# Attention and channel mix on one core: q and k loaded as 16-bit by GpSimd and turned on VectorE, scores in 32x64 tiles, a new order

## The chip, the cores and the metric

The kernel runs on one core of a Trainium2 chip. A core has a matrix engine (TensorE, PE in the profile, with its weight loads on a row of their own, PEld), VectorE (DVE), ScalarE (ACT), GpSimd (POOL), SyncE (SP), and 16 DMA engines that move data between the chip's memory (HBM) and the core's on-chip memory. TensorE reads on-chip memory (SBUF) and writes PSUM, eight banks of 512 32-bit numbers for each of 128 partitions. The metric is the device time of one execution in microseconds (us), lower is better. The kernel before took 272.23 us, the median of three executions of 269.08, 272.96 and 272.23 us.

## The reference

Eight batches of eight heads of blockwise causal attention (576 positions, 64 numbers per head, blocks of 64 positions), and then a channel mix (RWKV style) on the 512 joined channels. Cut to what matters:

```python
scores = scale * np.matmul(q, k.transpose(0, 1, 3, 2))        # (8, 8, 576, 576)
mask = pos[:, None] // 64 >= pos[None, :] // 64
attn = softmax(np.where(mask, scores, -1e9))
x = np.matmul(attn, v)      # heads joined: (8, 576, 512)
x_prev = x shifted by one position
xk = mu_k * x + (1 - mu_k) * x_prev
xr = mu_r * x + (1 - mu_r) * x_prev
k = np.maximum(xk @ w_k, 0)             # 512 -> 1024
out = sigmoid(xr @ w_r) * (k * k @ w_v) # 1024 -> 512
```

All inputs and the output are 32-bit; the tensors q, k and v are 9.4 MB each and the output as much.

## The kernel before

Every engine executes its own list of instructions in order, and waits on the others through semaphores. The lists are written by hand: a plan holds tasks with their buffers (`RINGS` gives the number of buffers of each kind), the table `ORDER` gives the order in which the tasks are issued, and the string `PLACE` says which of DVE, ACT and POOL does a task that any of them could do.

Attention of one batch has these stages.

- **Load and turn.** TensorE needs q and k with the head dimension on the partitions. Batches 0 to 3 (`LONGS`) load long rows of 2304 bytes (`add_long`, 288 KB a transfer), cast them to bf16 into `t_nl`, transpose 64x64 blocks on TensorE against the identity (L371) into PSUM, and copy these to `t_qkt` (L262, L268). Batches 4 to 7 load rows of 256 bytes (`add_qk`), cast them into `t_nb`, and transpose them by DMA (L318). The values v are loaded and cast into `t_vo` (`add_v`).
- **Scores.** `add_scores` multiplies k by q, transposed, into `t_s` (three PSUM buffers of two banks). From batch 1 on, a unit of four heads is made of matmuls on 64x64 tiles of the array (L489), four of them on different quarters. ACT takes the exponential into `t_e` (L517, 1024 or 640 numbers a partition). Batch 0 has units of its own, with 64x128 tiles (L499).
- **Values.** `add_av` sums the exponentials (S, L577) and multiplies them by the values (T, A and B, L586: 64x32 tiles), in `t_s` buffers too. DVE turns the sums (L620), takes reciprocals (L626), turns those back (L634), and scales the result into `t_xt` (norm, L642 and L650). Batch 0 has two groups with a form of their own (`add_av0`).
- **Mix.** `add_mix` makes x minus x_prev (L742, or L739 on ACT) and from it `t_xk` and `t_xr` (L766, L770), laid out in chunks of 512 positions. 576 is not a multiple of 512, so most mixes are split in two.

The channel mix runs over nine chunks of 512 positions (c), in PSUM buffers `t_mm` (two banks): `add_pk` (L794: 8 times 4 matmuls of 128x128 by 512 columns, relu at L804 or L806, square at L812 or L814), `add_pr` (L828, tanh at L836), `add_pv` (L854, product at L864, store at L872). TensorE's instructions at L279 (`unread`) are matmuls whose result nobody reads, put in by `ORDER` at the start and in the first 40 us. SP issues every load, store and DMA transpose, 181 rows in all.

## Time and profile before

| | before |
|---|---|
| executions | 269.08, 272.96, 272.23 us (median 272.23) |
| span of the profiled execution | 269.2 us (its own time is not given apart; the span equals the fastest of the three) |
| PE busy | 247.1 us (92%), 3700 matmuls |
| DVE busy | 196.7 us (73%) |
| ACT busy | 184.8 us (69%) |
| POOL busy | 92.3 us (34%) |
| SP's DMA queue | 110208 packets, 75.5% of 16 engines' span |
| chain that ended last | PE 62%, DMA 13%, DVE 8%, ACT 7%, SP's issuing 4% |

An engine's busy time is the time in which any of its instructions runs; instructions overlap, so the sum over groups is larger than that. The chain that ended last follows the work back from the last instruction to what released it. "Window" below is a stretch of the span, in us from its start. The median of the executions is 3.0 us above the span.

### The profile page before, as it was taken

How to read it: one execution, taken by the hardware profiler on the slowest of the kernel's cores; microseconds unless marked ns; L12 is line 12 of the kernel's file. 1: busy time of each engine (PE TensorE's matmuls, PEld its weight loads, DVE VectorE, ACT ScalarE, POOL GpSimd, SP SyncE). 2: the span in 40 equal slices, each digit the busy share in tenths (PEclk: the TensorE clock that was granted, in tenths of full speed). 3: DMA queues.
4: the chain of work that ended last, by engine and by line, in shares of the span. 5: the costliest groups of instructions: out<-in, count | busy, mean ns of one | idle time of the engine just before them, and what ended most of it. 6: DMA issues, size and time to landing. Idle time of an engine off the chain costs nothing.

```text
span 269.2 us, 8792 instructions
## 1 busy us (share of the span) xinstructions
PE 247.1 (92%) x3700; PEld 123.4 (46%) x3700; DVE 196.7 (73%) x354; ACT 184.8 (69%) x270; POOL 92.3 (34%) x123
## 2 busy tenths in 40 slices
PE   7879779899899996789899999699999999999995
PEld 3544336444446444334354445345444544444442
DVE  1597696999888976266968969588985599943432
ACT  4869588788786885399569886695788563661440
POOL 3555614731337311365155103413403350140310
PEclk9988799999999999999999999999999999999999
DMA  7999997899999697998999899889932201202213
GB/s 217 391 205 315 268 228 209 261 259 228 220 239 223 166 226 162 207 209 225 201 198 225 195 223 207 199 192 219 194 104 78 80 4 39 80 0 79 78 56 144
DMA packets 110249, 48.83 MB, mean 181 GB/s; under 512 B 98816, under 2 KB 99072, under 8 KB 110208
## 3 DMA queue, kind: packets, MB, share of 16 engines
q1 hardware_dynamic: 110208, 48.25, 75.5%
q8 instruction: 29, 0.48, 0.8%
q14 instruction: 12, 0.10, 0.1%
HBM read 33.56 MB, written 9.44 MB: 160 GB/s over the span
## 4 chain that ended last, share of the span: by engine, by line
PE 62%; DMA 13%; DVE 8%; ACT 7%; SPq 4%; issue 3%; POOL 1%; DVEq 0%; ACTq 0%; POOLq 0%
PE t_mm L854 18%; PE t_mm L794 15%; PE t_mm L828 10%; PE t_s L489 5%; PE t_s L586 5%; DMA t_vl<-in_v_dram 4%; ACT t_e L517 4%; SPq L251 4%; DMA out_dram<-t_o 2%; DMA t_ld<-in_q_dram 2%; PE t_s L577 2%; DMA t_qkt<-t_nb 2%; PE t_s L371 2%; DMA t_ld<-in_k_dram 2%; ACT t_kr L804 2%
## 5 line engine op out<-in xcount | busy, mean ns | idle before, releaser
L517 ACT ACTIVATE t_e<-t_s 128x1024 f16<-128x1024 f32 (+1 forms) x96 | 88.9, 977 | 15.4 <-PE t_s L489 13.4
L794 PE MATMUL t_mm<-t_xk,WK 128*128 128x512 f16 x288 | 67.8, 379 | 4.1 <-ACT t_kr L804 2.7
L854 PE MATMUL t_mm<-WV,t_k 128*128 128x512 f16 (+1 forms) x296 | 66.4, 374 | 0.2 <-DVE t_k L814 0.2
L804 ACT ACTIVATE t_kr<-t_mm 128x512 f32<-128x512 f32 x61 | 36.2, 599 | 29.2 <-PE t_mm L794 23.1
L814 POOL TENSOR_TENSOR t_k<-t_kr 128x512 f16<-128x512 f32 x26 | 29.0, 1128 | 60.5 <-ACT t_kr L804 36.8
L794 PEld LDWEIGHTS <-WK 128*128 128x128 f16 x288 | 26.7, 97 | 37.0 <-issue 8.2
L854 PEld LDWEIGHTS <-t_k 128*128 128x128 f16 x296 | 27.7, 98 | 33.8 <-issue 2.3
L864 DVE SCALAR_TENSOR_TENSOR t_o<-t_t,t_mm 128x512 f32<-128x512 f32 (+1 forms) x37 | 24.8, 670 | 20.4 <-PE t_mm L854 13.0
L828 PE MATMUL t_mm<-WR,t_xr 128*128 128x512 f16 x144 | 35.9, 379 | 0.7 <-ACT t_kr L804 0.7
L770 DVE SCALAR_TENSOR_TENSOR t_xk<-t_d,MUK,t_xt 128x384 f16<-128x384 f32 (+7 forms) x56 | 30.8, 563 | 7.2 <-POOL t_d L742 7.2
L770 DVE SCALAR_TENSOR_TENSOR t_xr<-t_d,MUR,t_xt 128x384 f16<-128x384 f32 (+7 forms) x56 | 32.7, 599 | 0.0
L836 ACT ACTIVATE t_t<-t_mm 128x512 f32<-128x512 f32 x36 | 21.4, 598 | 16.1 <-PE t_mm L828 13.3
L489 PE MATMUL t_s<-t_qkt 64*64 64x64 bf16 (+7 forms) x560 | 25.4, 291 | 3.3 <-DMA t_qkt<-t_nb 3.3
L742 POOL TENSOR_TENSOR t_d<-t_xt 128x576 f32<-128x576 f32 x16 | 19.0, 1193 | 23.7 <-DVE t_xk L770 12.0
L814 DVE TENSOR_TENSOR t_k<-t_kr 128x512 f16<-128x512 f32 x24 | 18.1, 755 | 8.5 <-ACT t_kr L804 8.4
L586 PE MATMUL t_s<-t_e,t_vo 64*32 64x64 f16 (+7 forms) x1120 | 20.8, 284 | 1.1 <-POOL t_vo L268 1.1
L828 PEld LDWEIGHTS <-t_xr 128*128 128x128 f16 x144 | 13.5, 97 | 17.8 <-issue 3.0
L489 PEld LDWEIGHTS <-t_qkt 64*64 64x64 bf16 x560 | 12.4, 106 | 17.5 <-issue 10.2
L268 POOL CAST t_vo<-t_vl 128x576 f16<-128x576 f32 (+1 forms) x17 | 12.9, 761 | 20.9 <-DMA t_vl<-in_v_dram 20.9
L586 PEld LDWEIGHTS <-t_vo 64*32 64x32 f16 x1120 | 14.6, 92 | 9.1 <-issue 3.2
L268 DVE COPY t_qkt<-t_s 128x576 bf16<-128x576 bf16 x18 | 13.1, 752 | 7.3 <-PE t_s L371 6.6
L268 POOL CAST t_nl<-t_ld 128x576 bf16<-128x576 f32 x18 | 11.8, 666 | 19.0 <-DMA t_ld<-in_k_dram 13.4
(73 smaller groups left out, 242.5 us busy)
## 6 DMA issues: line engine op xcount, KB each, us to landing
out_dram<-t_o SPq DMA_DIRECT2D x35, 256.0 KB, 2.9
t_vl<-in_v_dram SPq DMA_DIRECT2D x56, 144.0 KB, 4.2
t_ld<-in_q_dram SPq DMA_DIRECT2D x16, 288.0 KB, 5.5
t_ld<-in_k_dram SPq DMA_DIRECT2D x16, 288.0 KB, 5.3
t_ld<-in_q_dram SPq DMA_DIRECT2D x32, 128.0 KB, 3.5
t_ld<-in_k_dram SPq DMA_DIRECT2D x32, 128.0 KB, 3.7
t_ld<-in_moe_w_k_dram SPq DMA_DIRECT2D x8, 256.0 KB, 6.0
t_ld<-in_moe_w_v_dram SPq DMA_DIRECT2D x8, 256.0 KB, 4.0
```

Of the source, the lines that this page charges most:

```text
L268: e.tensor_copy(dst, src)
L489: nc.tensor.matmul(PS[y * D:y * D + D, x, col:col + n], kq[:, 1, t * D:t * D + D], kq[:, 0, q0:q0 + n], start=True, stop=True)
L517: nc.scalar.activation(new(ebuf)[:, :, 0:w], new(m)[:, :, 0:w], AF.Exp, scale=ISQ)
L586: nc.tensor.matmul(PA[out, u, HALF + f * D:HALF + f * D + D] if kind == "T" else PA[out, u, lo - D:lo - D + n], weight((b, rows, c, t % JT ...
L770: nc.vector.scalar_tensor_tensor(dst, dt[:, 0, lo:lo + w], (MUK1, MUR1)[n][:, cc:cc + 1], x, ALU.mult, ALU.add)
L794: nc.tensor.matmul(ps, WK[:, cc, jc * P:(jc + 1) * P], new(tiles["xkb", c])[:, cc], start=(cc == 0), stop=(cc == CCn - 1))
L804: nc.scalar.activation(kt, ps, AF.Relu)
L814: (nc.vector if eng == "DVE" else nc.gpsimd).tensor_tensor(dst, KR, KR, ALU.mult)
L828: nc.tensor.matmul(ps, xr[:, cc, jt * P:(jt + 1) * P], WR[:, cc], start=(cc == 0), stop=(cc == CCn - 1))
L836: nc.scalar.activation(new(tb), new(m), AF.Tanh, scale=0.5)
L854: nc.tensor.matmul(ps[:, 0:w], k2[:, jc, jt * P:(jt + 1) * P], WV[:, jc, cols], start=(jc == 0), stop=(jc == JCn - 1))
L864: nc.vector.scalar_tensor_tensor(new(o)[:, 0:w], new(tiles["tbf", c, jt])[:, cols], 1.0, new(m)[:, 0:w], ALU.add, ALU.mult)
```

## The change

The attention part is written anew, the channel mix keeps its matmuls, and all of `ORDER`, `PLACE` and `RINGS` is new (code lines of the changed kernel have numbers of their own).

- **q and k.** A transfer is a group of four heads of q or k, 128 partitions of 1152 numbers (576 KB), four of them a batch. From batch 1 on GpSimd issues it and it casts to bf16 on the way (`nc.gpsimd.dma_start`, L274, 28 transfers), into one of five `t_nb`. Batch 0 is loaded by SP (L283, each transfer in two) and cast by DVE or POOL.
- **Turn.** VectorE transposes 32x32 blocks of 4 bytes, each two neighbouring bf16 (L292, 32 instructions of 128x576 32-bit numbers). So partitions hold pairs of the head dimension: a group's four heads lie on four strips of 32 partitions, and the two numbers of a pair lie side by side. TensorE's and the DMA's transposes and the copies out of PSUM are gone, and `identb` is read by nothing.
- **Scores.** A score is the sum of two matmuls (f = 0 and 1) on 32x64 tiles, whose operands step by two numbers (L396). A unit has all eight heads and fills both `t_s` buffers; two exponentials follow (L417). In batches 0 and 1 (`SPLIT`) a unit is two tasks of four heads each.
- **Values.** `t_s` has two buffers (three before), and one buffer `t_av` of two banks takes S and T, A and B in turn. `t_xt` has one buffer (two before), `t_nb`, `t_e` and the others as in `RINGS`.
- **Batch 0 by thirds** of 192 positions (`add_third`): scores, sums, values, norm and mix of a third, and the first chunk of the channel mix in pieces of 192, 192 and 128 columns (`SUBS`).
- **Mixed inputs.** `t_xk` and `t_xr` are one buffer each of two batches (1152 positions), used in a circle. A mix writes 576 positions at once; where a chunk of 512 goes over the end, `add_pk` does two matmuls in place of one (chunks 2, 4 and 6).
- v comes in two loads a batch (four before), weights in larger pieces. No unread matmuls are left.

```diff
-    RINGS = {"ld": 8, "vl": 4, "nl": 8, "nb": 4, "tl": 1, "qkt": 2, "e": 13,
-             "xt": 2, "tt": 1, "rc": 2, "rt": 1, "d": 2, "xk": 3, "xr": 2,
-             "kr": 3, "k2": 1, "t": 3, "o": 3, "s": 3, "mm": 2,
-             "vo": 2}
+    RINGS = {"ld": 6, "nb": 5, "qkt": 2, "vo": 2, "e": 9, "xt": 1, "tt": 1,
+             "rc": 2, "rt": 1, "d": 2, "xk": 2, "xr": 2, "kr": 4, "k2": 2,
+             "t": 4, "o": 3, "s": 2, "av": 1, "mm": 2}
...
+        if b in DIRECT:
+            t = add(f"qkld {b} {g} {n}", ("POOL",),
+                    lambda eng, me: nc.gpsimd.dma_start(
+                        new(nb), rows(GH * g, GH)),
+                    uses=[nb], kind="ldc", kb=P * LW * 4 / 1024)
...
+        def turn(eng, me):
+            nc.vector.transpose(
+                new(qkt)[:, n, g].rearrange("p t e -> p (t e)").bitcast(
+                    FP).rearrange("p (r j) -> p j r", r=RW),
+                new(nb)[:, :].bitcast(FP).rearrange(
+                    "p (j s) -> p j s", s=RW))
...
-                for col, t, q0, n in BLOCKS[it[1]]:
-                    for y in range(2):
-                        for x in range(2):
-                            rows = slice(x * D, x * D + D)
-                            kq = qkt[rows, it[0] + 2 * y]
-                            nc.tensor.matmul(
-                                PS[y * D:y * D + D, x, col:col + n],
-                                kq[:, 1, t * D:t * D + D],
-                                kq[:, 0, q0:q0 + n], start=True, stop=True)
+            for col, t, q0, n in pieces:
+                for f in range(2):
+                    for y in range(2):
+                        for a in heads:
+                            g, at = place(b, a, y)
+                            rows = slice(at * QC, at * QC + QC)
+                            nc.tensor.matmul(
+                                new(ms[a // 2])[y * D:y * D + D, a % 2,
+                                                col:col + n],
+                                qkt[rows, 1, g, t * D:t * D + D, f],
+                                qkt[rows, 0, g, q0:q0 + n, f],
+                                start=f == 0, stop=f == 1,
+                                tile_position=(at * QC, y * D))
...
+    THIRDS = [
+        [[(0, 0, 0, 192), (192, 1, 64, 128), (320, 2, 128, 64)]],
+        [[(0, 0, 192, 192), (192, 1, 192, 192), (384, 4, 256, 128)],
+         [(0, 2, 192, 192), (192, 3, 192, 192), (384, 5, 320, 64)]],
...
+        at = (c * CH + lo) % XW
+        n = min(w, XW - at)
+        parts = [(0, n, at)] + ([(n, w - n, 0)] if n < w else [])
```

Three places of the new order follow, before and after (names: `t_e` exponentials, `t_kr` relu of the channel mix, `t_ld` a load, `t_nl` and `t_nb` bf16 q or k, `t_qkt` turned q and k).

ACT, around its first relu of the channel mix. Before:

```order
L517 ACTIVATE t_e_158<-t_s_187 128x2x320
L517 ACTIVATE t_e_159<-t_s_186 128x1024
L517 ACTIVATE t_e_160<-t_s_187 128x1024
L262 COPY t_qkt_148<-t_s_188 128x576
L262 CAST WK<-t_ld_129 128x512
L262 CAST WK<-t_ld_124 128x512
L262 COPY t_qkt_148<-t_s_188 128x576
L804 ACTIVATE t_kr_176<-t_mm_189 128x512
```

and in the changed kernel:

```order
L417 ACTIVATE t_e_129<-t_s_156 128x1024
L417 ACTIVATE t_e_128<-t_s_155 128x2x320
L417 ACTIVATE t_e_128<-t_s_156 128x2x320
L417 ACTIVATE t_e_127<-t_s_155 128x1024
L223 CAST t_vo_125<-t_ld_115 128x1152
L674 ACTIVATE t_kr_143<-t_mm_159 128x192
L683 ACTIVATE t_k_146<-t_kr_142 128x192
```

In both, 24 exponentials (batches 0 and 1) stand ahead of the first relu; the casts and copies of q and k among them are gone, and the relu has 192 columns.

DVE at the start of the program. Before, after its memsets:

```order
L268 CAST t_nl_137<-t_ld_125 128x576
L268 COPY t_qkt_148<-t_s_187 128x576 x2
L268 COPY t_qkt_148<-t_s_188 128x576 x2
L268 CAST t_nl_135<-t_ld_125 128x576
L268 CAST t_nl_136<-t_ld_124 128x576
```

and in the changed kernel, where `t_nb_117`, `_118` and `_119` are at first GpSimd's transfers for batch 1 and `t_qkt_122` is batch 0:

```order
L229 CAST t_nb_121<-t_ld_111 128x1152
L292 STREAM_TRANSPOSE t_qkt_122<-t_nb_121 128x18x32
L292 STREAM_TRANSPOSE t_qkt_123<-t_nb_117 128x18x32
L229 CAST t_nb_117<-t_ld_112 128x1152
L292 STREAM_TRANSPOSE t_qkt_122<-t_nb_117 128x18x32
L229 CAST t_nb_117<-t_ld_113 128x1152
L292 STREAM_TRANSPOSE t_qkt_122<-t_nb_117 128x18x32
L292 STREAM_TRANSPOSE t_qkt_123<-t_nb_118 128x18x32
```

The turn that TensorE and ACT did is now in DVE's list, and a turn of batch 1 stands between the casts of batch 0's q and k.

POOL in the middle of its list. Before, it had casts and squares (`t_k`):

```order
L268 CAST t_nl_138<-t_ld_127 128x576
L814 TENSOR_TENSOR t_k_179<-t_kr_178 128x512
L268 CAST t_nb_145<-t_ld_123 128x512
L268 CAST t_nb_145<-t_tl_147 64x2x128
L268 CAST t_nl_136<-t_ld_126 128x576
L814 TENSOR_TENSOR t_k_179<-t_kr_176 128x512
```

and in the changed kernel transfers and squares:

```order
L274 DMA t_nb_119<-in_k_dram 128x1152
L274 DMA t_nb_120<-in_k_dram 128x1152
L274 DMA t_nb_121<-in_q_dram 128x1152
L274 DMA t_nb_118<-in_k_dram 128x1152
L685 TENSOR_TENSOR t_k_146<-t_kr_145 128x128
L274 DMA t_nb_117<-in_q_dram 128x1152
L685 TENSOR_TENSOR t_k_147<-t_kr_142 128x512
```

The loads of q and k have moved from SP's list into POOL's, where a transfer that waits for its `t_nb` holds up the squares behind it. SP's list goes from 181 rows to 71.

More of the change, by code (lines that the diff above doesn't have):

```diff
@@ L455 @@
+    WHOLE = [
         [(0, 0, 64, 512)],
@@ L781, with mixed_in, add_pk @@
+    def mixed_in(n, lo, hi):
+        return ([t for a, z, t in mixed[n] if a < hi and z > lo],
+                [mix_buf[b][n] for b in range(B)
+                 if b * S < hi and (b + 1) * S > lo])
     act = {}
-    def add_pk(c, jc):
+    SUBS = {0: [(0, 192), (192, 384), (384, 512)]}
+    def add_pk(c, jc, lo, hi):
         m, kr = plan.buf("mm"), plan.buf("kr")
-        if jc == 0:
+        if ("k2b", c) not in tiles:
             tiles["k2b", c] = plan.buf("k2")
         k2b = tiles["k2b", c]
+        w = hi - lo
+        at = (c * CH + lo) % XW
+        n = min(w, XW - at)
+        parts = [(0, n, at)] + ([(n, w - n, 0)] if n < w else [])
@@ L845, in add_pv @@
         g = c * CH + jt * P
+        k2s = [act["k2", c, jc, lo] for jc in range(JCn)
+               for lo, hi in SUBS.get(c, [(0, CH)])
+               if lo < jt * P + P and hi > jt * P]
         for half in range(halves):
```

841 lines of the change are left out of this document (353 added, 488 removed), and 118 rows, old and new, of tables (ORDER, THIRDS).

## The prediction

> **What bounds the kernel now.** The page first, for the engines' shares and, in 40 slices, TensorE and the DMA engines.
>
> ```profile
> span 269.2 us, 8792 instructions
> PE 247.1 (92%) x3700; PEld 123.4 (46%) x3700; DVE 196.7 (73%) x354; ACT 184.8 (69%) x270; POOL 92.3 (34%) x123
> ...
> PE   7879779899899996789899999699999999999995
> ...
> DMA  7999997899999697998999899889932201202213
> GB/s 217 391 205 315 268 228 209 261 259 228 220 239 223 166 226 162 207 209 225 201 198 225 195 223 207 199 192 219 194 104 78 80 4 39 80 0 79 78 56 144
> ```
>
> TensorE carries the span, beside DMA engines that are full until slice 30. Then the stages: a first that ends where the channel mix begins (42.1, from the chain below), one in which attention and mix are mixed, one almost of mix alone, and the last product and store.
>
> ```profile
> core 0: us, PE busy (x) PEld busy (x) DVE busy (x) ACT busy (x) POOL busy (x), PEclk, DMA share, GB/s
> 0.00:42.10 42.10, 34.77 (x797) 19.43 (x798) 26.87 (x64) 30.88 (x38) 20.43 (x44) 0.92 1.00 269
> 42.10:200.00 157.90, 146.23 (x2350) 72.95 (x2348) 128.72 (x224) 119.93 (x181) 56.37 (x67) 1.00 0.96 210
> ...
> 100.00:120.00 20.00, 15.05 (x295) 7.75 (x294) 9.29 (x15) 12.50 (x22) 8.20 (x10) 1.00 0.90 191
> ...
> 200.00:266.10 66.10, 66.05 (x559) 30.98 (x556) 40.70 (x67) 34.01 (x52) 15.47 (x13) 1.00 0.16 59
> 266.10:269.20 3.10, 0.00 (x0) 0.00 (x0) 0.41 (x1) 0.00 (x0) 0.00 (x0) 1.00 0.34 127
> ```
>
> So the span is 42.1 us of ramp, 146.2 + 66.1 = 212.3 us of TensorE work, 11.7 us in which TensorE idles (157.9 − 146.2) and 3.1 us of end. 5.0 of the 11.7 lie in 100 to 120 alone. Who was waited for there is in the chain:
>
> ```profile
> 2.13 5.23 DMA t_ld<-in_k_dram
> ...
> 42.13 2.71 PE t_mm L794 x12
> ...
> 102.56 0.63 SPq L251
> 103.24 0.62 SPq L251
> 103.92 2.06 SPq L251
> 107.18 0.63 SPq L251
> 107.85 4.34 DMA t_vl<-in_v_dram
> ```
>
> SP issues loads one by one, and a late load of v ends there. The change can gain by a shorter ramp, by less TensorE work and by fewer such holes; the end stays.
>
> **The ramp.** In both kernels 24 exponentials of batches 0 and 1 stand on ACT ahead of its first relu. What they cost, from the windows of L517 alone (ACT busy, instructions, clock, DMA), and the casts that stay among them, from the groups by line:
>
> ```profile
> 0.00:42.10 42.10, 22.50 (x24) 0.92 1.00 269
> ```
>
> ```profile
> L262 ACT CAST t_vo<-t_vl 128x576 f16<-128x576 f32 x6 | 4.1, 675 | 0.8 <-DMA t_vl<-in_v_dram 0.8
> L262 ACT CAST WK<-t_ld 128x512 f16<-128x512 f32 x3 | 1.8, 637 | 0.0
> ```
>
> The timeline has the first of them at 8.2:
>
> ```profile
> 8.19 1.94 ACT L517 ACTIVATE t_e<-t_s 128x1024 f16<-128x1024 f32 x2 [0.48 <-PE t_s L499]
> ```
>
> The 24 have 23808 numbers a partition before and 23040 after (18 of 1024, and two each of 768, 896 and 640): 21.8 us. Two casts of 1152 are four times 0.675, the one of 1024 twice 0.637: 4.0 us. Together 25.8, where ACT was busy 30.9 before; six copies and casts of q and k are what is gone.
>
> They start later, though. At 8.2 was 0.8 us after the chain's k had landed (7.36, the last of four 288 KB transfers: as much as group 0 of q and k now). Behind that landing now stand a cast of 1152 and a turn, before a score:
>
> ```profile
> L268 DVE CAST t_nl<-t_ld 128x576 bf16<-128x576 f32 x8 | 4.3, 552 | 5.5 <-DMA t_ld<-in_q_dram 5.1 <-DMA t_ld<-in_k_dram 0.4
> L634 DVE STREAM_TRANSPOSE t_rt<-t_rc 128x576 f32<-128x576 f32 x14 | 10.2, 759 | 0.2
> ```
>
> Twice 0.55, 0.76 and 0.5 for the score make 2.4: 9.7. GpSimd's five transfers of batch 1 share the DMA engines; at half of them k would land 5.2 later, at 12.6, and the first exponential at 14.9. I take 11.5, nearer the first since GpSimd's five must be issued one after another. Then ACT is done at 37.3, with some gaps at **38**, instead of 42.1: 4 us. DVE's own first relu stands behind twelve turns (9.1), four casts (4.3) and the sums, norms and first mixes of the thirds; from 6 on that is 20 without the latter, which wait for exponentials in their turn, so I let ACT set the end of the ramp. Without the unread matmuls the clock may stay low in the ramp; ACT covers that.
>
> **TensorE's work behind the ramp.** At the first mix matmul both kernels stand alike: batch 0 done, batch 1's scores done. From there the transposes go, the scores change and the mix gets pieces. First the windows of L371 alone and of L489 alone (PE, PEld), then rows of the timeline, then groups by line:
>
> ```profile
> 42.10:269.20 227.10, 5.06 (x219) 4.24 (x216) 1.00 0.72 165
> 42.10:269.20 227.10, 20.88 (x480) 10.38 (x480) 1.00 0.72 165
> ```
>
> ```profile
> 53.21 0.76 PE L371 MATMUL t_s<-identb,t_nl 64*64 64x64 bf16 x36 [1.20 <-DVE t_xt L650]
> 53.90 1.39 PE L586 MATMUL t_s<-t_e,t_vo 64*32 64x512 f16 x72
> ```
>
> ```profile
> L489 PE MATMUL t_s<-t_qkt 64*64 64x64 bf16 (+7 forms) x560 | 25.4, 291 | 3.3 <-DMA t_qkt<-t_nb 3.3
> L794 PEld LDWEIGHTS <-WK 128*128 128x128 f16 x288 | 26.7, 97 | 37.0 <-issue 8.2
> ```
>
> - Transposes (first row, L371): −5.1.
> - Scores (second row, L489): 480 instructions become 960, as eight tiles work at once in place of four, so the columns per time are equal. The trace has no 32x64 tile. The nearest, also eight at once, is L586: 72 in 1.39 us, 19 ns each, 18.5 us in all; the old score's 25.4/560 = 45 ns gives 43.5. I take no change (22 ns), near the first. Range: −2.4 to +22.6.
> - Pieces: 160 more matmuls in `add_pk`. By columns they cost nothing; if a weight load (97 ns) is not hidden, a 128-column piece (a quarter of 0.22) loses 42 ns, one of 192 some 15 ns: 96 x 42 + 64 x 15 = 5 us. I take 3.
>
> Together 212.3 − 5.1 + 3 = **210.2**. The Trainium skill speaks against the scores here: "TensorE: Matmul & The Clock Gate", in its section on 56 ns against 53.3, puts the least start-to-start of matmuls at about 25 ns; by it 960 would take 24 us, and the sum would be 3 us more. The trace does not bear that floor out: 36 of L371 went in 0.76 us, 21 ns each.
>
> **DVE, POOL and DMA behind it,** by groups of lines and shapes:
>
> ```profile
> L268 DVE COPY t_qkt<-t_s 128x576 bf16<-128x576 bf16 x18 | 13.1, 752 | 7.3 <-PE t_s L371 6.6 <-ACT t_e L517 0.6
> L268 DVE CAST t_nb<-t_ld 128x512 bf16<-128x512 f32 x15 | 6.2, 419 | 3.1 <-DMA t_qkt<-t_nb 1.8 <-DMA t_ld<-in_q_dram 1.0 <-DMA t_ld<-in_k_dram 0.2
> L806 DVE TENSOR_SCALAR t_kr<-t_mm 128x512 f32<-128x512 f32 x11 | 7.5, 686 | 3.1 <-PE t_mm L794 3.1
> L814 DVE TENSOR_TENSOR t_k<-t_kr 128x512 f16<-128x512 f32 x24 | 18.1, 755 | 8.5 <-ACT t_kr L804 8.4
> L770 DVE SCALAR_TENSOR_TENSOR t_xk<-t_d,MUK,t_xt 128x64 f16<-128x64 f32 x6 | 2.0, 333 | 0.0
> ```
>
> DVE loses copies (13.1), casts of q and k (6.2 + 4.3) and nine squares (6.8), and gains 32 turns of 0.76 (24.3), three casts (3.3) and nine relus with eleven narrow ones (6.2 + 4). 128 mix products become 80: 48 times the fixed part of some 0.27 (0.333 for 64 columns), −13. So it falls by about 5; if a turn that writes with a step takes twice as long, it rises by 20, from 197 to 217. In 42 to 200 DVE was busy 129 of 158, so the one is covered and the other would show.
>
> POOL gets 28 issues. SP's take 0.39 to 1.8 us (timeline), and 288 KB land in 5.3 us (page):
>
> ```profile
> 0.75 0.39 SPq L251 DMA_DIRECT2D t_ld<-in_q_dram  x1
> 98.62 1.82 SPq L318 DMA_TRANSPOSE t_qkt<-t_nb  x1
> ```
>
> ```profile
> t_ld<-in_k_dram SPq DMA_DIRECT2D x16, 288.0 KB, 5.3
> ```
>
> 11 to 51 us on an engine that is busy 92 of 269; its casts of q and k go. Cover: buffers of `t_kr` and `t_k`. The DMA engines lose the DMA transposes and the 256-byte rows of q and k.
>
> The single `t_av` adds a wait: the product A starts only when S is turned, inverted, turned back and T scaled, three turns of 0.76 and two smaller steps on DVE, some 3 us. In TensorE's order 24 or more matmuls of the mix (2.6 us even where they are halves) and a unit of scores stand between; if that cover is too short, all that follows on TensorE waits. Scores likewise need both exponentials of the unit before (2 us), with 1.8 to 4.4 us of mix between. I let this cost what the smaller holes leave: of 11.7 idle the 5.0 of late loads go, **7** stay (bounds 3 and 16).
>
> **Sum:** 38 + 210.2 + 7 + 3.1 = 258.3 of span, against 269.2. The median is 3.0 above the span, so **261 us**, 4% less.
>
> **Rivals.**
>
> *Better* (span below 252): first exponential at 9.7, so a ramp of 36.2; idle 3; pieces free: 36.2 + 207.2 + 3 + 3.1 = 249.5 of span, 252.5 us. For it: all engines but TensorE get lighter. Chance 0.14.
>
> *No gain but the order* (267 span, 270 us): the ramp stays at 42.1 and the idle at 11.7: 42.1 + 210.2 + 11.7 + 3.1. For it: 2.36 MB of batch 0 and 2.95 MB of batch 1 start at once, and a turn of batch 1 stands ahead of batch 0's k on DVE. The Trainium skill has a mechanism for a late ramp, "SBUF — State Buffer", who interferes with whom: a VectorE copy or cast in a two-port mode keeps GpSimd from writing its transfers' descriptors. The cast of 512 in 0.419 us against a turn of 576 in 0.759 shows such a fast mode; three casts at the start could hold up the transfers by 3.3 us. Chance 0.20 with all causes.
>
> *Slower: 32-row tiles don't run eight at once*, or a step of two slows the operand. At the old score's 45 ns the 960 instructions add 22.6: 281 span, 284 us. It decides from (20.9 + 10.9)/960 = 33 ns on, where the gain is used up. Against it: L586 has eight tiles at 19 ns. Chance 0.10.
>
> *Slower: the casting transfers set the pace.* No row shows one. Twice 5.3 us for 576 KB, one behind the other, makes 28 x 10.6 = 297, far over 300 us in all; at 6.7 each they just keep up with a last batch at 190, at 7.5 the end comes 22 later, about 280 span. POOL's blocked squares would do the same. Against it: 391 GB/s in the page's second slice. Chance 0.08.
>
> **Numbers.** The forecast, 252 to 263 of span, has 0.48. A change of 2% (5.4 us) is about what a measurement of this kernel can tell. Faster by more, below 266.8: 0.48 + 0.14; within 2%: 0.20; slower: 0.18. The range goes from the better case with the scores at 19 ns to most of the slow scores: 249 to 281; some 0.18 stays out.
>
> **What would show it.** The first relu at 36 to 40; score instructions at 19 to 25 ns; TensorE's idle between ramp and 200 below 10; turns at 0.76 us; DMA share well below 0.9 after the ramp. A first exponential behind 15, turns of 1.5 us, or POOL waiting on `t_nb` with squares behind it would make it wrong.

## The result, and the profile after

The changed kernel takes **286.16 us** (four executions, 283.0 to 286.35), against 272.6 us for the kernel before beside it (269.08 to 273.16): a ratio of 1.057, 95% interval 1.048 to 1.067. It is slower by 5 to 7%, where 261 us were predicted. The profiled execution took 286.35 us, with a span of 284.6; the text below is about that span. In four experiments below one or two of the four executions took over 1.5% longer than the fastest: times and ratios are those of the others, but two profiles (the turn without a step, values first with the clock kept) are of such a longer execution.

From the page of the changed kernel: the span, the engines' shares, and in 40 slices of 7.1 us TensorE, its granted clock and the DMA engines.

```profile
span 284.6 us, 9493 instructions
...
PE 247.6 (87%) x4232; PEld 136.8 (48%) x4232; DVE 197.6 (69%) x288; ACT 175.3 (62%) x252; POOL 84.1 (30%) x105
...
PE   0056865795889999999999999999999999999995
...
PEclk9998575577799999999999999999999999999999
DMA  7999999576999998898238012003001200300123
```

TensorE is busy as long as before (247.6 against 247.1) but the span is 15.4 longer, and the gaps stand in the first twelve slices; in eight of these (the fourth to the eleventh) the clock was granted at 0.8 or less as well. The windows of the forecast's stages, cut at the first score (16.39) and the first mix matmul (56.02):

```profile
core 0: us, PE busy (x) PEld busy (x) DVE busy (x) ACT busy (x) POOL busy (x), PEclk, DMA share, GB/s
0.00:16.39 16.39, 0.00 (x0) 0.00 (x1) 7.46 (x12) 1.28 (x1) 3.55 (x11) 1.00 0.93 217
16.39:56.02 39.63, 27.74 (x845) 20.68 (x846) 19.75 (x37) 23.11 (x25) 9.45 (x14) 0.68 1.08 214
56.02:80.00 23.98, 19.46 (x338) 13.52 (x337) 17.33 (x38) 17.28 (x34) 10.31 (x16) 0.75 0.77 166
80.00:200.00 120.00, 119.25 (x2132) 61.99 (x2130) 104.55 (x135) 89.81 (x124) 44.15 (x49) 1.00 0.60 123
200.00:281.20 81.20, 81.14 (x924) 40.65 (x922) 48.13 (x68) 43.85 (x68) 16.67 (x15) 1.00 0.14 52
281.20:284.60 3.40, 0.00 (x0) 0.00 (x0) 0.40 (x1) 0.00 (x0) 0.00 (x0) 1.00 0.32 116
```

From 80 us on TensorE idles 0.8 us in 201: nothing was to be gained there. The ramp ends at 56.02, against 42.13 before and 38 in the forecast; that is 13.9 of the 15.4. Where it goes is told by the same ramp cut at the end of the twelfth exponential (30.20), and by what TensorE waited for behind it:

```profile
17.51:30.20 12.69, 9.74 (x312) 7.92 (x308) 5.42 (x9) 11.96 (x13) 4.19 (x6) 0.87 1.15 242
30.20:56.02 25.82, 16.88 (x513) 11.63 (x510) 13.30 (x27) 11.14 (x13) 5.26 (x8) 0.57 1.05 201
```

```profile
PE t_s L396 <- issue: 3.9, 2, 2.5
PE t_av L568 <- issue: 3.5, 2, 2.8
```

The first dozen exponentials runs as forecast: 12.7 us, ACT busy 12.0 of them. The second dozen takes 25.8, in which ACT is busy 11.1 only. Now TensorE is the long list: 16.9 us busy, mostly at half the clock (0.57), and 7.4 us of "issue" (the columns are the sum, the number and the longest), in which it waited for nothing that these views show. The chain has these stalls in the middle of the value products of batch 0 (L568):

```profile
6.89 8.30 SPq L314
...
15.24 3.91 SPq L252
...
21.36 13.92 DMA t_ld<-in_v_dram
...
37.78 2.48 issue
40.26 0.66 PE t_s L396 x5
40.92 2.19 PE t_av L568 x118
43.12 2.79 issue
...
56.02 1.39 PE t_mm L661 x8
```

SP stood 8.3 and 3.9 us at single loads (DMA share 0.93 and 1.08 in the windows), so the second half of batch 0's v was asked for at 21.4 and landed at 35.3. Between the stalls at 37.78 and 43.12 the timeline has 5 matmuls of L396 and 123 of L568, 128 with 128 weight loads. DMA queue 8 ("instruction") brings 0.54 MB in 33 packets through the same engines: some 16 KB each.

The same trace says when they came. These are that queue's rows in four stretches of 0.1 us (29.9:30.0, 37.1:37.2, 42.8:42.9 and 47.6:47.7; a packet counts where it starts). The last figure is the time of the one packet as a share of 16 engines, so the packets took 0.96, 1.51, 1.48 and 1.29 us:

```profile
q8 instruction: 1, 0.02, 60.1%
q8 instruction: 1, 0.02, 94.3%
q8 instruction: 1, 0.02, 92.2%
q8 instruction: 1, 0.02, 80.9%
```

They had landed at some 30.9, 38.7, 44.3 and 49.0, and TensorE's four stalls ended at 32.42, 40.26, 45.91 and 50.46, each some 1.5 us later. It is so in every kernel here: each stall of 0.6 us or more in the first 84 us, the two of the kernel before among them, ends 1.2 to 1.8 us behind the landing of such a packet. TensorE was waiting for its instructions.

### The profile page after: what moved, and what is told of

Its sections match the earlier page's. It is cut to its first block, busy times and chain, and to the rows that moved or that the text cites. A ratio compares the mean times of both kernels' runs of the same rounds, so it can differ in the third digit from the quotient of the medians.

```text
span 284.6 us, 9493 instructions
## 1 busy us (share of the span) xinstructions
PE 247.6 (87%) x4232; PEld 136.8 (48%) x4232; DVE 197.6 (69%) x288; ACT 175.3 (62%) x252; POOL 84.1 (30%) x105
## 3 DMA queue, kind: packets, MB, share of 16 engines
q1 hardware_dynamic: 45904, 26.49, 38.7%
q0 software_dynamic: 4032, 8.26, 17.1%
## 4 chain that ended last, share of the span: by engine, by line
PE 79%; SPq 7%; DMA 5%; issue 4%; ACT 3%; DVE 1%; POOL 0%; DVEq 0%; ACTq 0%; POOLq 0%
PE t_mm L661 24%; PE t_mm L730 21%; PE t_mm L700 12%; PE t_s L396 9%; PE t_av L491 7%; DMA t_ld<-in_v_dram 5%; PE t_av L480 4%; SPq L314 3%; PE t_av L568 2%; SPq L283 2%; ACT t_e L417 2%; SPq L252 2%; DVE t_kr L676 1%; ACT t_kr L674 1%; POOL t_vo L229 0%
## 5 line engine op out<-in xcount | busy, mean ns | idle before, releaser
L417 ACT ACTIVATE t_e<-t_s 128x1024 f16<-128x1024 f32 (+3 forms) x96 | 89.3, 968 | 45.8 <-PE t_s L396 45.1
L661 PE MATMUL t_mm<-t_xk,WK 128*128 128x512 f16 (+4 forms) x448 | 72.9, 313 | 1.9 <-DVE t_kr L676 1.3
L396 PE MATMUL t_s<-t_qkt 32*64 32x192 bf16 (+7 forms) x1424 | 43.9, 308 | 26.2 <-DVE t_qkt L292 16.4
L685 POOL TENSOR_TENSOR t_k<-t_kr 128x512 f16<-128x512 f32 (+2 forms) x41 | 37.0, 913 | 84.8 <-ACT t_kr L674 50.8
L661 PEld LDWEIGHTS <-WK 128*128 128x128 f16 x448 | 39.9, 101 | 30.6 <-issue 8.4
L396 PEld LDWEIGHTS <-t_qkt 32*64 32x64 bf16 x1424 | 25.6, 115 | 43.8 <-issue 23.7
L674 ACT ACTIVATE t_kr<-t_mm 128x512 f32<-128x512 f32 (+2 forms) x57 | 30.1, 531 | 20.1 <-PE t_mm L661 18.5
L292 DVE STREAM_TRANSPOSE t_qkt<-t_nb 128x576 f32<-128x576 f32 x32 | 38.2, 1243 | 1.9 <-POOL t_nb L229 1.8
L608 POOL TENSOR_TENSOR t_d<-t_xt 128x576 f32<-128x576 f32 (+1 forms) x17 | 16.9, 999 | 52.8 <-DVE t_xk L628 19.4
L528 DVE TENSOR_TENSOR t_xt<-t_av,t_rt 128x1024 f32<-128x1024 f32 x14 | 17.1, 1221 | 8.1 <-PE t_av L491 8.1
L491 PE MATMUL t_av<-t_e,t_vo 64*32 64x512 f16 (+7 forms) x1120 | 21.8, 284 | 0.2 <-issue 0.2
L628 DVE SCALAR_TENSOR_TENSOR t_xr<-t_d,MUR,t_xt 128x576 f16<-128x576 f32 (+1 forms) x29 | 20.8, 722 | 0.6 <-POOL t_d L608 0.6
L628 DVE SCALAR_TENSOR_TENSOR t_xk<-t_d,MUK,t_xt 128x576 f16<-128x576 f32 (+1 forms) x29 | 19.9, 690 | 0.2
L491 PEld LDWEIGHTS <-t_vo 64*32 64x32 f16 x1120 | 14.4, 92 | 10.9 <-issue 5.7
```

The costliest lines, as they stand in the source:

```text
L292: nc.vector.transpose(new(qkt)[:, n, g].rearrange("p t e -> p (t e)").bitcast(FP).rearrange("p (r j) -> p j r", r=RW), new(nb)[:, :].bitca ...
L396: nc.tensor.matmul(new(ms[a // 2])[y * D:y * D + D, a % 2, col:col + n], qkt[rows, 1, g, t * D:t * D + D, f], qkt[rows, 0, g, q0:q0 + n, f ...
L417: nc.scalar.activation(new(e)[:, 2 * h:2 * h + 2, 0:w], new(ms[h])[:, :, 0:w], AF.Exp, scale=ISQ)
L491: nc.tensor.matmul(PA[o, u, HALF + f * D:HALF + f * D + D] if kind == "T" else PA[o, u, lo - D:lo - D + n], weight(b, u, c, t % JT, f), E[ ...
L628: e.scalar_tensor_tensor(dst, dt[:, 0, 0:W], (MUK1, MUR1)[n][:, cc:cc + 1], x, ALU.mult, ALU.add)
L661: nc.tensor.matmul(ps[:, a:a + n], WK[:, cc, jc * P:(jc + 1) * P], MIX[0][:, cc, at:at + n], start=(cc == 0), stop=(cc == CCn - 1))
```

## Experiments

Each kernel ran in three rounds against the kernel before, so ratios carry some 1% of uncertainty and two neighbours with a few tenths between them are the same. The kernels ran in batches on several chips, so a difference of 1 to 3 us between batches rests on the moments in the traces as much as on the times. The moments are those of one execution, whose time is up to 1.5 us from the one in the table (4.1 with the clock kept). All edits are to the changed kernel's table of tasks, unless code is shown. The table sums up, in us: first exponential, first value product, first mix matmul, first product with w_v (the last point of the start: behind it the changed kernel and all but two of its variants take 202.0 to 203.4 us, the kernel before 211.4), and the median time.

| | exp | value | mix | w_v | time |
|---|---|---|---|---|---|
| before | 8.2 | 22.7 | 42.1 | 57.8 | 272.6 |
| changed | 17.5 | 36.0 | 56.0 | 82.0 | 286.2 |
| v first | 18.3 | 35.7 | 54.3 | 80.9 | 285.4 |
| k in order | 14.8 | 35.8 | 52.5 | 78.4 | 283.2 |
| many unread matmuls | 18.4 | 42.7 | 62.3 | 89.2 | 294.5 |
| batch 2 late | 18.2 | 37.9 | 55.7 | 82.2 | 286.7 |
| unread, own buffer | 18.8 | 36.5 | 53.5 | 79.4 | 285.6 |
| same, k in order | 14.3 | 35.2 | 53.8 | 80.6 | 284.0 |
| same, v first, batch 2 late | 14.4 | 38.7 | 55.6 | 81.1 | 284.0 |
| order of need | 11.5 | 36.0 | 52.9 | 78.9 | 283.1 |
| order of need, half the values | 11.4 | 35.7 | 48.4 | 74.7 | 279.7 |
| order of need, quiet DMA | 12.4 | 36.6 | 47.4 | 90.5 | 297.3 |
| order of need, nothing unread | 11.7 | 35.7 | 53.8 | 79.8 | 283.8 |
| values first | 11.4 | 22.2 | 46.8 | 82.5 | 286.1 |
| values first, clock kept | 11.7 | 22.7 | 49.6 | 82.8 | 290.6 |
| same, SP held back | 11.5 | 22.5 | 46.3 | 82.8 | 287.9 |
| quiet, let go early | 11.6 | 35.9 | 49.3 | 79.2 | 283.3 |
| fewer bytes | 15.7 | 35.0 | 50.6 | 76.6 | 279.9 |
| fewer bytes, unread | 16.0 | 34.0 | 47.7 | 73.7 | 280.1 |

### One transfer, one order, one clock at a time

v first: task 17 is the second half of batch 0's v, 21 and 19 are pieces of w_k, 1 the mu vectors.

```diff
-3 0 124 12 6 122 9 120 15 126 21 4 5 19 1 179 125 13 14 17 7 8 23 62 123 89 63
+3 0 124 12 6 122 9 120 15 17 126 4 5 21 179 125 13 14 19 1 7 8 23 62 123 89 63
```

> The second half of batch 0's v is loaded right behind the first half, ahead of two pieces of w_k and of the mu vectors; nothing else moves. Theory A (the order of the transfers in full DMA engines sets when batch 0's data land, and the first value product waits for this half, which landed at 35.3): it lands some 8 to 10 us earlier, the first mix matmul comes at 47 to 51 instead of 56.0, and the time falls by 5 to 9 us, to 277 to 281. Theory B (TensorE's low clock in the first 80 us sets the ramp): less than 2 us. Theory C (the list of casts and turns on VectorE and of exponentials on ScalarE sets the ramp): no change, 285 to 287.

Measured 285.4 (ratio 1.065, 1.056 to 1.074): theory A's 5 to 9 us didn't come. This half of v was there 3.6 us earlier (its cast began at 31.8 in place of 35.4), the wait for it went, and the chain shows what was behind it: TensorE's own work, from a k that lands no earlier (14.9; in the changed kernel its cast began at 14.3).

```profile
3.92 11.00 DMA t_ld<-in_k_dram
...
17.15 1.09 PE t_s L396 x21
18.27 1.03 ACT t_e L417
...
41.50 2.17 issue
...
54.34 1.39 PE t_mm L661 x8
```

k in order: the loads 12 and 6, the casts 13 and 7 and the turns 14 and 8 change places (group 1 and group 0 of batch 0's k).

> Group 0 of batch 0's k is loaded, cast and turned before group 1, which the first score doesn't need. Theory A: the first score, at 16.4, and the first exponential, at 17.5, come 2 to 4 us earlier; the end of the ramp moves by less than 1 us as long as the second half of v lands at 35. Theory C (ScalarE's 24 exponentials run from the first of them on without large gaps): all of the 2 to 4 us show in the time, 282 to 284.

Measured 283.2 (1.056, 1.048 to 1.064): the first exponential 2.8 earlier, the first mix matmul 3.4, the time 3.0. By the ratio, 1.056 for 1.057, it would be nothing; but the other orders on this chip took 285.4 and 286.7, and the first product with w_v agrees (3.6 earlier). v's second half landed at 34.9, as before, and did not hold the gain back: the time is theory C's. That ScalarE ran without large gaps, as C had it, is not so.

Many unread matmuls: 124 of them, 30 at the start and the others mostly two ahead of a task (and 12 ahead of the first value product), with a line that lets them write the tasks' own buffers from the first sums on.

> Unread matmuls are put in as the kernel before had them: 30 at the start and 2 to 12 behind many TensorE tasks up to some 80 us. Theory B (without them TensorE's clock stays low, 0.68 in 16 to 56 and 0.75 in 56 to 80): the granted clock in 16 to 80 is above 0.9, the stretch from the first mix matmul to 80 us shortens, and the time falls by 5 to 9 us, to 277 to 281. Theories A and C: the clock rises, but in the ramp TensorE waits anyway; only the 5 us or less behind the ramp are gained, less what the unread matmuls take, so 0 to 4 us.

Measured 294.5 (1.101, 1.088 to 1.114). The clock rose as theory B has it (0.88 in 16 to 56, 0.93 in 56 to 80), but PE's busy time rose by 23.7 us, 9.3 of it ahead of 16 us where TensorE had idled, and the first mix matmul came at 62.3, 6.3 later. What was put on TensorE behind the first score cost more than the clock gave back; how much of that is TensorE's time and how much the exponentials' buffers that these matmuls took, this run doesn't tell.

Batch 2 late: GpSimd's tasks 179, 185, 181, 183 and 232 behind the cast of v's second half.

> GpSimd's casting transfers of batch 2 and the first of batch 3, issued before 24 us, are issued behind the cast of the second half of batch 0's v. Theory A (these transfers take their share of the full DMA engines, 1.7 us of all sixteen for each): batch 0's v lands 5 to 8 us earlier, the first mix matmul comes at 48 to 51, and the time falls by 4 to 8 us, unless batch 2 then comes late. Theories B and C: no change or slower by what batch 2 comes late.

Measured 286.7 (1.071, 1.063 to 1.079): no gain. v's second half did land 7 us earlier (its cast began at 28.2 in place of 35.4), as theory A has it, but k landed at 14.9, no earlier, and the first value product came later, not earlier. Late v is not what ends the ramp.

### Together

One mm buffer is held for the unread matmuls until the last score of batch 1:

```diff
-                         uses=([ms[h]] if split else ms) + [qkt_buf[b]],
+                         uses=([ms[h]] if split else ms) + [qkt_buf[b]]
+                         + [wbuf] * (b in SPLIT),
```

> Unread matmuls again, but so that they can take no exponential's buffer: they write one mm buffer that is held until batch 1's last score, 54 at the start (up to about the first score, 16.4) and one ahead of each of the next twelve score tasks. Theory D (TensorE runs the ramp at half speed because it stood idle up to 16 us: 24 score matmuls of a third took 1.09 us in the runs without unread ones and 0.58 in the one with many): scores and values of the ramp take about half, the ramp becomes that of ScalarE's 25.8 us behind the first exponential at 17.5, the first mix matmul comes at 44 to 49, and the time falls by 7 to 12 us, to 274 to 279. Rival E (the many unread matmuls of the other run cost what they gained because such a matmul always delays the path): no gain, 284 or more.

> As the run before it, and group 0 of batch 0's k ahead of group 1, with 42 unread matmuls at the start. Theory D: the gains add up, since ScalarE's list then starts 3 us earlier: first mix matmul at 41 to 46, 271 to 276. If the second half of batch 0's v (35 us) now ends the ramp: first mix matmul at 44 to 49, as without the new order of k.

> As the run before it, and the second half of batch 0's v right behind the first half, and GpSimd's transfers of batch 2 behind v's cast. Theory D with the transfers as second bound: v no longer ends a wait, first mix matmul at 40 to 43, 268 to 273, level with the kernel before. If ScalarE's list alone sets the ramp by now: as without these two moves, within 1 us.

Measured 285.6, 284.0 and 284.0 (1.067, 1.059, 1.059). Scores of a third fell from 1.09 to 0.6 for a while, and it was worth 0 to 2 us: the first dozen exponentials paces the scores at either speed, and behind it the clock fell again (in the third of these kernels two of the stalls are 2.9 and 2.5 us). Rival E's time came.

Order of need: batch 0's q, k and v first; GpSimd's 124, 122, 120 and 126 (batch 1) behind its cast 10, and VectorE's turns of batch 1 behind those of batch 0. A number behind a plus sign is that of the unread matmuls ahead of the task.

```diff
-3 0 124 12 6 122 9 120 15 126 21 4 5 19 1 179 125 13 14 17 7 8 23 62 123 89 63
...
+3 0+34 6 12 9 15 17 4 5 21 7 8 13 14 19 1 23 62+1 89+1 63 90 93+1 10 124 122
+120 126 94 39+1 11 125 25 40 97+1 121 98 123 66+1 67 91+1 16 41+1 42 187 92
...
```

> Transfers in the order of need: SP loads batch 0's q and k (group 0 of k first) and both halves of its v; GpSimd's four transfers of batch 1 stand behind its cast of batch 0's last q, those of batch 2 behind v's cast; VectorE's turns of batch 1 behind those of batch 0; 34 unread matmuls at the start and twelve later, in a buffer of their own. Theory A2 (the bytes of batch 1 and 2 that are in the engines beside batch 0's are what delays it): the first exponential comes at 9 to 12 in place of 17.5, the first mix matmul at 38 to 46, and the time is 268 to 276. Rival F (behind the first value product it is TensorE's own supply of instructions, its stalls of 2 to 3 us in the profile, that sets the pace, 16 to 18 us from there to the first mix matmul in every run so far): the first exponential comes early, but the stretch from the first value product on still takes 16 to 18 us, and less than half of the 6 us is gained at the end.

> As the run before it, but the second half of batch 0's value products (f = 1) is made for the first key block alone: 176 matmuls in place of 304, so batch 0's values are wrong. Theory F: 256 instructions of TensorE less are half as many stalls; the stretch from the first value product to the first mix matmul shrinks by 4 to 6 us, of which the work itself is 2.5 (128 at 19 ns). If the stretch is set by something else (ScalarE's exponentials): by less than 2.

> As the first of these, but batch 2's q, k and v, the first of batch 3 and w_v are loaded behind GpSimd's first x minus x_prev of batch 0's last third, and all later loads but those of v of batch 1 by GpSimd, so that the DMA engines are nearly empty from 35 us up to the first mix matmul. Theory F2 (the stalls are instruction transfers that queue in full DMA engines): the stalls of 2 to 3 us shrink below 1, and the stretch from the first value product to the first mix matmul by 4 to 6 us; batch 2 comes late behind it and may give all of it back. If a stall is as long with empty DMA engines, the fetch itself sets it.

> As the first of these without any unread matmul. Theory D (half speed while TensorE is cold): scores of a third at 1.1 us in place of 0.6 up to the first value product, first mix matmul 2 to 5 us later. If exponentials or transfers set the ramp: within 1 us.

Measured: order of need 283.1 (1.045, 1.037 to 1.053), half the values 279.7 (1.031, 1.022 to 1.041; it leaves out 128 products, so batch 0's values are wrong), quiet 297.3 (1.096), nothing unread 283.8 (1.048). The first exponential came at 11.54, and the ramp still ended at 53: rival F. Its chain (GpSimd's last transfer of batch 1, three turns, then the stalls):

```profile
15.81 10.64 DMA t_nb<-in_q_dram
26.48 3.43 DVE t_qkt L293 x3
...
38.85 1.98 issue
...
43.38 2.55 issue
...
52.96 1.39 PE t_mm L665 x8
```

With 128 value matmuls less the stretch from first value product to first mix matmul fell from 16.9 to 12.7 us, and 3.4 of that reached the end. Of the 4.2 us 2.9 are stalls (2.3 us in place of 5.2), the rest is mostly the products' own time. With empty DMA engines the waits of TensorE in 32 to 52, and the windows of that kernel (the second one is TensorE waiting for batch 2):

```profile
PE t_av L572 <- issue: 0.9, 1, 0.9
```

```profile
32.00:48.00 16.00, 12.92 (x535) 9.58 (x528) 9.19 (x26) 11.98 (x14) 4.75 (x9) 0.82 0.08 10
48.00:64.00 16.00, 3.85 (x71) 2.64 (x69) 3.41 (x7) 1.31 (x4) 8.56 (x14) 0.61 1.04 226
```

At a DMA share of 0.08 all 304 value matmuls ran with one stall of 0.9 us, in place of 4.5 + 0.7 in 32 to 53 of the order of need at 1.02, and the first mix matmul came 5.5 us earlier. So full DMA engines lengthen the wait for instructions. They are not all of it: in the order with SP held back, below, a stall of 1.6 us (36.2 to 37.8) stands where the DMA share is 0.15, so that it isn't known what a fetch costs by itself.

```profile
34.80:37.80 3.00, 1.43 (x114) 1.32 (x96) 2.93 (x10) 0.00 (x0) 0.00 (x0) 0.86 0.15 28
```

Without any unread matmul: theory D's 2 to 5 us didn't come, 0.9 at the mix.

The same 16.9 us laid beside the wait for batch 1 (batch 0's sums and values ahead of batch 1's scores, its first mixes too), then the same with full-size unread matmuls kept on, then that with SP held back behind the norm of the last third; and the quiet order with batch 2 let go at 39 to 41 us:

> The order of need once more, with the wait for batch 1's q and k (TensorE idle from 22.6 to 28.9) filled: batch 0's sums and value products, its norms and first mixes stand ahead of batch 1's scores, batch 0 third by third, and the first four tasks of the channel mix between batch 1's last scores; v of batch 1 is loaded ahead of w_v and of v of batch 2. Theory G (the ramp is two waits one behind the other, for the data of batch 1 and for TensorE's instructions in the value products, and neither is ScalarE's list): laid beside each other they cost once; the last of batch 1's exponentials ends at 44 to 48 in place of 54, the span falls by 5 to 9 us, 274 to 278. Rival (the transfers alone set it: batch 1's and 2's and the weights' bytes must be in before the mix gets going, in any order): less than 2 us, 281 to 283.

> The values-first order with unread matmuls of full size kept on through the stretch in which the clock was granted at 0.50 (26 to 76 us) though TensorE was busy nearly all of 43 to 58: one or two ahead of each sum and value product of batch 0 and one ahead of each of batch 1's twelve scores, in the same buffer, held until the last of them. Theory D2 (small tiles don't bring the clock back, matmuls of the whole array do; at half speed a score of batch 1 takes 1.07 us in place of 0.59 and a task of the mix 0.75 in place of 0.40): the granted clock in 24 to 60 rises above 0.8, batch 1's scores and the first mix tasks take 6 to 9 us less, the 20 or so matmuls cost 4 to 5, and the time falls by 3 to 6 us, to 280 to 283. Rival (the stalls for instructions leave TensorE idle and so cold whatever is put between): clock stays at 0.5 to 0.6, 286 to 288.

> As the run before it, and SP waits for the norm of batch 0's last third (by a copy of a few numbers that reads its result) before it loads w_v and v of batch 2, and GpSimd's transfers of batch 2 stand behind its first x minus x_prev and its casts of w_k. Theory F2 (the stalls are instruction transfers queueing in full DMA engines): the stalls in the value products, 1.6 + 3.0 + 1.8 + 2.4 us, fall to half or less, and with them the time by 3 to 5 us more, to 275 to 280, as long as batch 2's q and k, asked for at about 35, land ahead of their scores at 45 to 50. Rival: in 22 to 35 the engines are still full with batch 1 and w_k, the stalls stay, and the late batch 2 costs 2 to 6 us.

> The order of need with batch 1's scores ahead of batch 0's values, as in the run with the quiet DMA engines, but what was held back there is let go as soon as the values need no more instructions: GpSimd's transfers of batch 2 behind its first two x minus x_prev of batch 0 (about 39 us), SP's loads of w_v and of v of batch 2 behind the norm of batch 0's last third (about 41). Theory F2: the DMA engines are empty from 32 to 39, the value products run without stalls of over 1 us, the first mix matmul comes at 47 to 49 as in the quiet run, and with batch 2 landing at 46 to 50 the gain of 7 to 9 us reaches the end: 276 to 280. Rival H (the 8 us are given back at once, since batch 2's q and k come later by as much): the first mix matmul as early, TensorE idle between 52 and 62, 283 to 288.

Measured 286.1 (1.060, 1.052 to 1.067), 290.6 (1.080), 287.9 (1.068), 283.3 (1.052, 1.045 to 1.059). None of these paid, so theory G falls. Values first has its first mix matmul at 46.8, 9 us earlier than the changed kernel, and its first product with w_v no earlier at all: the stalls stayed (1.6, 3.0, 1.8, 2.4), and from 44 to 58 TensorE was busy nearly all the time at half the clock.

```profile
44.00:58.00 14.00, 13.43 (x198) 7.49 (x191) 6.22 (x10) 9.59 (x12) 2.55 (x5) 0.50 0.76 151
```

Nor did unread matmuls of the whole array bring the clock back there (expected above 0.8). This is a window of the third kernel, which has the same unread matmuls; one of them comes every 1.5 us or so, with a group of scores of batch 1 in between that takes 1.07 us (0.65 ahead of 38.9, at the full clock).

```profile
40.00:52.00 12.00, 12.00 (x107) 4.47 (x99) 4.33 (x10) 7.17 (x7) 4.26 (x7) 0.50 0.95 181
```

In the last of the four, where one stall was 0.8 us (DMA share 0.47 in 32 to 40) and the next 2.8 (1.10 in 42 to 49), the mix started at 49.3, 3.6 earlier than in the order of need, and the time was the same. What comes next is VectorE, with turns of batch 2 and mixes of batch 0 in one list; 8.9 of these 10 us it is busy:

```profile
58.00:68.00 10.00, 6.94 (x76) 4.38 (x75) 8.93 (x19) 7.13 (x11) 4.66 (x8) 0.67 1.05 198
```

### The bytes alone, and the turn

Fewer bytes: the changed kernel's own order, eight transfers cut short.

```diff
+        W = D if b in (1, 2) else LW
...
-                        new(nb), rows(GH * g, GH)),
+                        new(nb)[:, 0:W], rows(GH * g, GH)[:, 0:W]),
```

> The changed kernel in its own order, with the eight casting transfers of batches 1 and 2 cut to an eighteenth (64 of 1152 numbers a partition, the rest of each buffer stays zero, so the scores of batches 1 and 2 are wrong): 4.5 MB less to move in the first 50 us, and not one instruction of TensorE, VectorE or ScalarE less. Theory A+F (the full DMA engines set the start, by late data and by late instructions): the first exponential comes at 10 to 13, v's second half at 18 to 24, the stalls shrink below 1 us each, the first mix matmul comes at 42 to 47 in place of 56, the first product with w_v at 66 to 73 in place of 82, and the time falls by 9 to 16 us, to 270 to 277. Rival L (the engines' own lists and TensorE's low clock set it, and the order in which they wait for each other): first product with w_v at 76 or later, 280 or more.

> As the run before it with the unread matmuls of the fifth experiment (54 at the start, one ahead of each of twelve score tasks). Theory D3 (with the transfers out of the way TensorE's half speed is what is left of the ramp): 3 to 6 us less than the run before it. Theory A+F alone: within 2 us, or slower by what the 54 hold up, since the first score now comes earlier than their end.

Measured 279.9 (1.042, 1.035 to 1.050) and 280.1 (1.044, 1.035 to 1.053): 6.2 us less (4.1 by the ratios), at rival L's edge; the unread matmuls added nothing to that. The stalls fell from 7.4 to 3.1 and the mix came 5.4 us earlier, but the first product with w_v still at 76.6, 19 behind the kernel before. So some 4 to 6 of the 13.6 us are bytes. That the rest is in the engines' lists follows by exclusion and isn't shown by a run of its own. The second dozen of exponentials took 22.5 us here, with TensorE busy 17.8; then a row of its timeline, and the same products in the changed kernel:

```profile
28.20:50.68 22.48, 17.81 (x549) 12.59 (x541) 13.09 (x24) 12.10 (x14) 4.11 (x7) 1.00 0.74 154
```

```profile
37.22 2.26 PE L571 MATMUL t_av<-t_e,t_vo 64*32 64x192 f16 x123
```

```profile
40.85 2.27 PE L568 MATMUL t_av<-t_e,t_vo 64*32 64x192 f16 x123
```

The changed kernel had a granted clock of 0.5 there, so this kernel's 1.00 isn't its speed: its trace has no record of the clock ahead of 54.0, and the row counts time without a record as 1.00. It gained its 4 to 6 us with TensorE no faster.

The turn:

```diff
-                    FP).rearrange("p (r j) -> p j r", r=RW),
+                    FP).rearrange("p (j r) -> p j r", r=RW),
```

> The changed kernel, but the 32 turns write their result in one piece in place of a step of 18 numbers (the positions come out in another order, so the output isn't the reference's). Theory T (the stepped write makes a turn 1.24 us in place of 0.76): turns of 0.75 to 0.80 us, VectorE's sum falls by 15 us to 182, and the time by 0.5 to 2.5 us, for the four turns ahead of the first exponentials. Rival U (reading in steps of 32 numbers costs it): turns stay at 1.24, no change.

Measured 286.2 (1.069, 1.050 to 1.088): no change in the time. The row of the turn in the changed kernel, and then in this one:

```profile
L292 DVE STREAM_TRANSPOSE t_qkt<-t_nb 128x576 f32<-128x576 f32 x32 | 38.2, 1243 | 1.9 <-POOL t_nb L229 1.8
```

```profile
L292 DVE STREAM_TRANSPOSE t_qkt<-t_nb 128x576 f32<-128x576 f32 x32 | 23.5, 759 | 3.2 <-POOL t_nb L229 2.8
```

Theory T's price is right: the stepped write costs 0.48 us a turn, 15 us of VectorE in all. Its 0.5 to 2.5 us of time aren't seen; the turns are covered.

## Why the prediction was wrong

**The ramp, 38: measured 56.02. This is the step that failed,** in the sentence "so I let ACT set the end of the ramp". Two things went into it. (The span was missed by 26.3 us, 284.6 for 258.3: 18.0 here, 9.65 in TensorE's work behind.)

- *The first exponential, 11.5: measured 17.51.* Group 0 of k is the third load of SP, behind group 1, and landed at 14.3, beside all of batch 1's bytes, where my bounds were 7.36 and 12.6; the cast, turn and score behind it took 3.2 for 2.4. The 11.54 of the order of need is no proof of my 11.5: there GpSimd's transfers start at 14.6, the case for which I had 9.7. Putting k right gave 3.0 us of time.
- *Then ACT's 25.8 us of exponentials and casts: measured 38.5.* The first dozen took 12.7, as summed. The second took 25.8 because TensorE's list was the longer one: the scores of batch 1, the last sum and all values of batch 0, 16.9 us busy, and 7.4 of stalls. I summed ACT's list and the head of VectorE's and never TensorE's. "The clock may stay low in the ramp; ACT covers that" held for the first dozen (in the order of need eleven exponentials took 11.8 us with unread matmuls and 11.7 without) and not for the second.

The stalls were in the profile of before, as "issue" of 1.37 and 0.95 in the chain of its ramp, and nothing in my working asked what they were or what many more small matmuls would make of them.

**TensorE's work behind the ramp, 210.2: measured 219.85** (19.46 + 119.25 + 81.14 in the windows above), 9.65 over. By the windows of single lines (PE, PEld): scores (L396), tasks of the mix (L661), and the sums of batch 1 (L480), which stood ahead of the mix before:

```profile
56.02:284.60 228.58, 24.63 (x962) 12.12 (x960) 0.97 0.45 102
56.02:284.60 228.58, 72.82 (x448) 39.87 (x448) 0.97 0.45 102
56.02:80.00 23.98, 2.59 (x60) 1.84 (x60) 0.75 0.77 166
```

Scores 24.6 for 20.9 (+3.8), pieces 72.8 for 67.75 + 3 (+2.1), sums +2.6: at the first mix matmul the two kernels did not stand alike, as I had it. A part is the low clock up to 80 us, which the forecast had not carried beyond the ramp: there 98 scores took 4.11 us, 42 ns each, against 20.52 for 864 behind it, 23.8 ns. The rival of slow tiles (33 ns and more) is refuted. By the Trainium skill's least start-to-start of 25 ns ("TensorE: Matmul & The Clock Gate", section on 56 ns against 53.3) the 960 would have come to 24.0. The mean at the full clock is near it; but it is no floor here, as a row of the timeline has 32 in 0.49 us, 15 ns each:

```profile
84.66 0.49 PE L396 MATMUL t_s<-t_qkt 32*64 32x256 bf16 x32
```

**Idle, 7: measured 5.3,** 4.5 of it up to 80 us. Behind 80 us the single `t_av` and the units of eight heads cost 0.8 at most. **End, 3.1: 3.4.** Sum: 56.0 + 219.9 + 5.3 + 3.4 = 284.6. From span to time it is 1.75 in the profiled execution, not 3.0.

**Turns, 0.76: 1.24,** the case for which I had VectorE up by 20. The other savings took that back (197.6 for 196.7), and it costs no time. **GpSimd's transfers:** 0.57 us to issue, 17.1% of the engines' span for 28, 1.7 us of all sixteen each; behind 80 us the DMA share is 0.60 and less, so the rival of casting transfers that set the pace is refuted, but in the first 50 us they are a part of what is too much. POOL waited 21.8 us in all for a free `t_nb`, a sign that I had named; behind 80 us TensorE idled 0.8 all the same. The rival of a late ramp had 270 us, with the ramp at 42.1 as before; no rival allowed for a ramp later than that. VectorE's casts had no part in it at the start: GpSimd had issued batch 1's four transfers by 3.7 us, and the first cast stands at 6.6.

**What stays open:** how much of the second dozen is the half clock. Each attempt to keep the full clock either cost TensorE the same time or failed. Open too is how the rest of the 13.6 us, some 7 to 9, divides between TensorE's list and VectorE's behind it; no order tried here beat the kernel before.

## What to carry to other kernels

Where two engines feed each other through two buffers, sum both lists for each stretch, with the clock that the stretch has, and take the longer; a stretch in which one engine was covered before can be the other's now. Many small matmuls need instructions as fast as they run, and these come through the same DMA engines as the data: at 118 matmuls in 2.2 us beside full engines the stalls were 0.7 to 2.8 us, and they show only as "issue": lay their ends beside the packets of the instruction queue. At a start that several waits set side by side, taking one away tells its size in the time only after the others are gone: follow a point behind all of them (here the first product with w_v), not the end of one.

## What the runs showed of the hardware

- TensorE's speed isn't always told by the granted clock: 1.00 stands also where the trace has no record of it. In the order of need without unread matmuls (first fence: window and timeline) and with them (second) the window of 8 to 24 us has 1.00 in both, yet 48 score matmuls took 1.92 us in the one, 40 ns each, and 24 of the same took 0.65 in the other, 27 ns each. The first record of the clock in the one is at 18.4 us, in the other at 5.1:

```profile
8.00:24.00 16.00, 9.38 (x292) 8.30 (x292) 6.61 (x7) 10.91 (x12) 3.40 (x5) 1.00 1.16 240
...
10.61 1.92 PE L396 MATMUL t_s<-t_qkt 32*64 32x192 bf16 x48 [10.61 <-DVE t_qkt L292]
```

```profile
8.00:24.00 16.00, 13.42 (x317) 7.99 (x315) 6.56 (x6) 10.90 (x12) 3.39 (x5) 1.00 1.17 232
...
10.85 0.65 PE L399 MATMUL t_s<-t_qkt 32*64 32x192 bf16 x24
```

- The low clock outlasted 12 us of a TensorE that was busy all the time, with matmuls of the whole array in between (window 40 to 52 above). The Trainium skill, "TensorE: Matmul & The Clock Gate", in its part on the clock gate has the full clock return after some 3.4 us of sustained work; that agrees with the start of the order of need (7 unread matmuls took 2.64 us up to 4 us, 11 took the 2 us from 6 on) and not with this window, and no run here tells why.
- SP can stand 8.3 us in the issue of one load where the DMA engines are full, and all that it has to load later waits with it.
